# Transposing q and k of batches 2 to 7 by DMA instead of on TensorE, in an attention kernel fused with an expert layer

## Chip, cores, metric

One core of one Trainium2 chip. The metric is the device time of one launch in microseconds (us), the median of several executions. The profile is one execution, taken by the hardware profiler; its times count from the start of its own span.

## The reference

Sliding-window attention (window 128, ALiBi bias) over 8 batches of 8 heads, 576 positions, head size 64; its output, 4608 rows of 512, goes through a two-matrix layer with a gated activation.

```python
scores = (q @ k.T) / sqrt(64) + slope[h] * -(i - j)   # kept where 0 <= i - j < 128
x = softmax(scores) @ v                               # to rows of 512 = 8 heads x 64
h = x @ w_in                                          # 512 -> 2048
g = h * (1.0 / (1.0 + exp(-beta * h)))
out = g @ w_out                                       # 2048 -> 512, float32
```

## The kernel before

Each batch has five blocks of rows (128, 128, 128, 128, 64). A block of q and k is loaded as float32 rows into `fst`, cast to bf16 on GpSimd (`bst`), transposed on TensorE into PSUM, and copied by VectorE into `QK`, where the score matmuls read it. Batches alternate between two `QK` buffers. Each batch is done in two halves: blocks 0 to 2, then 3 and 4. GpSimd also casts v into `VS`.

```python
fst_pool = ctx.enter_context(tc.tile_pool(name="fst", bufs=16))
bst_pool = ctx.enter_context(tc.tile_pool(name="bst", bufs=4))
...
def load_qk(b, sb):
    rows = ROWS[sb]
    fq = load_rows(q, b, sb)          # nc.sync.dma_start, like every load and store here
    fk = load_rows(k, b, sb)
    t = bst_pool.tile([P, 2, H, D], BF16, name="bst", tag="bst")
    nc.gpsimd.tensor_copy(out=t[0:rows, 0], in_=fq[0:rows])
    c = nc.gpsimd.tensor_copy(out=t[0:rows, 1], in_=fk[0:rows])
    staged[b, sb] = t
...
def T(b, sb):
    rows = ROWS[sb]
    src = staged.pop((b, sb))
    tps = psum_t.tile([P, 2, NP, P], BF16, name="tps", tag="t")
    for i in range(2):
        for p in range(NP):
            nc.tensor.transpose(
                out=tps[:, i, p, :],
                in_=src[:, i, 2 * p : 2 * p + 2, :].rearrange("r h d -> r (h d)"),
                identity=ident[:],
            )
    nc.vector.tensor_copy(
        out=QK[b % 2][:, :, :, P * sb : P * sb + rows], in_=tps[:, :, :, 0:rows]
    )
...
def loads_ahead(b, m):
    if m == 0:
        if b:
            for sb in (3, 4):
                load_qk(b, sb)
            for sb in (2, 3, 4):
                load_v(b, sb)
    elif b + 1 < B:
        for sb in range(3):
            load_qk(b + 1, sb)
        for sb in range(2):
            c = load_v(b + 1, sb)
        if b == 0:
            ...                        # w_out, on another queue
```

TensorE's order is fixed by the program: for each group of 512 tokens, 16 steps `HS` (x by w_in into `hps`) alternate with 16 steps `OS` of the group before (`ops`), and pieces of the attention of the next group (transposes, scores `sps`, weights by v `pv`, transposes of x) are spread between them.

The softmax here doesn't subtract the row's maximum and nothing guards it: scores larger than these inputs give would overflow.

## Time and profile before

| | before |
|---|---|
| median time (3 runs) | 374.29 us |
| span of the profiled run (it took 376.31 us) | 374.6 us |
| first `ops` matmul on TensorE | 93.7 us |
| from there to the end | 280.9 us |
| q, k, v, weights read | 36.71 MB |

The prediction below shows how the profile is read: the slices for where the bound lies, the stretches for who sets the pace, the timeline for what a group costs. Three lines from the page and one from TensorE's timeline are added, because the result is measured against them.

```profile
PEclk9999999899999999999999999999999999999999
...
HBM read 36.71 MB, written 9.44 MB: 123 GB/s over the span
...
L96 POOL CAST bst<-fst 128x512 bf16<-128x512 f32 (+1 forms) x40 | 24.6, 615 | 108.8 <-issue 78.7
```

### The profile page before, as it was taken

What the parts mean: (1) busy time and instruction counts of PE and PEld (TensorE: products, weight loads), DVE (VectorE), ACT (ScalarE), POOL (GpSimd) and SP (SyncE); (2) the same over time, 40 slices, a digit from 0 to 9 for tenths busy, and PEclk for the clock granted to TensorE, in tenths of its full rate; (3) what the DMA queues carried; (4) which work ended last, traced back from release to release, by engine and by line L of the source; (5) the groups of instructions that cost most, each with busy time, mean ns of one, the idle gap of its engine ahead of it and who ended that gap; (6) DMA issues with size and microseconds to landing.
All of it is one profiled execution on the core that took longest, in us unless ns stands there. A gap on an engine that the chain in (4) does not pass through costs nothing.

```text
span 374.6 us, 6713 instructions
## 1 busy us (share of the span) xinstructions
PE 338.5 (90%) x2529; PEld 172.7 (46%) x2529; DVE 224.2 (60%) x473; ACT 214.4 (57%) x437; POOL 84.4 (23%) x151
## 2 busy tenths in 40 slices
PE   2367687788999999999999999999999999999995
PEld 1145334434454455445454545454545445544442
DVE  3266467777665677665666776776767755533400
ACT  1453359375745875585846694668566854445421
POOL 7570703453122213112033303320100000000000
PEclk9999999899999999999999999999999999999999
DMA  9999999999297898954138440000000010001012
GB/s 166 209 206 202 193 195 214 192 216 180 76 214 159 159 186 170 205 126 107 50 96 187 109 104 31 28 30 29 30 28 30 30 57 29 29 29 58 28 56 86
DMA packets 121985, 42.40 MB, mean 113 GB/s; under 512 B 113232, under 2 KB 117344, under 8 KB 121952
## 3 DMA queue, kind: packets, MB, share of 16 engines
q1 hardware_dynamic: 117728, 37.77, 47.9%
q0 software_dynamic: 4224, 4.19, 6.7%
q8 instruction: 20, 0.33, 0.4%
q14 instruction: 13, 0.11, 0.1%
HBM read 36.71 MB, written 9.44 MB: 123 GB/s over the span
## 4 chain that ended last, share of the span: by engine, by line
PE 80%; DMA 6%; DVE 4%; ACT 4%; SPq 4%; issue 1%; POOL 0%; ACTq 0%
PE ops L283 34%; PE hps L267 32%; PE sps L197 4%; DMA fst<-in_k_dram 4%; PE tps L171 4%; SPq L83 4%; ACT pt L207 3%; PE xt L249 2%; PE pv L233 2%; DVE gT L273 2%; PE pv L229 2%; DMA fst<-in_v_dram 1%; ACT sig L272 1%; DVE pt L211 1%; DVE qkT L176 1%
## 5 line engine op out<-in xcount | busy, mean ns | idle before, releaser
L272 ACT ACTIVATE sig<-hps,beta_h 128x512 bf16<-128x512 f32 x144 | 99.5, 692 | 98.4 <-PE hps L267 87.4
L267 PE MATMUL hps<-XT,W 128*128 128x512 bf16 x576 | 150.7, 385 | 3.6 <-DVE gT L273 3.0
L283 PE MATMUL ops<-W,gT 128*128 128x512 bf16 x576 | 144.9, 379 | 0.0
L273 DVE SCALAR_TENSOR_TENSOR gT<-sig,hps 128x512 bf16<-128x512 bf16 x144 | 98.3, 683 | 53.0 <-ACT sig L272 52.4
L207 ACT ACTIVATE pt<-sps,bias 128x256 bf16<-128x256 f32 (+2 forms) x256 | 100.4, 480 | 34.9 <-PE sps L197 34.6
L267 PEld LDWEIGHTS <-W 128*128 128x128 bf16 x576 | 51.1, 98 | 56.5 <-issue 10.9
L283 PEld LDWEIGHTS <-gT 128*128 128x128 bf16 x576 | 51.3, 98 | 52.2 <-issue 1.7
L211 DVE TENSOR_TENSOR pt<-pt,mask 128x1024 bf16<-128x1024 bf16 x64 | 46.1, 720 | 21.2 <-ACT pt L207 20.0
L96 POOL CAST bst<-fst 128x512 bf16<-128x512 f32 (+1 forms) x40 | 24.6, 615 | 108.8 <-issue 78.7
L197 PE MATMUL sps<-qkT 64*128 64x256 bf16 (+2 forms) x320 | 28.3, 271 | 14.1 <-ACT pt L207 13.1
L104 POOL CAST vs<-fst 128x512 bf16<-128x512 f32 (+1 forms) x40 | 26.1, 659 | 65.0 <-PE pv L233 38.1
L176 DVE COPY qkT<-tps 128x1024 bf16<-128x1024 bf16 (+1 forms) x40 | 25.5, 637 | 21.5 <-PE tps L171 21.3
L171 PE MATMUL tps<-ident,bst 128*128 128x128 bf16 x320 | 28.8, 240 | 7.8 <-POOL bst L96 4.3
L239 DVE TENSOR_TENSOR xn<-pv,zs 128x256 bf16<-128x256 f32 (+1 forms) x80 | 33.7, 422 | 2.6
L289 ACT ACTIVATE osb<-ops 128x512 f32<-128x512 f32 x36 | 21.6, 601 | 20.8 <-PE ops L283 20.8
L233 PE MATMUL pv<-vs,pt 128*128 128x65 bf16 x320 | 31.0, 200 | 2.5 <-DVE xn L239 1.5
L171 PEld LDWEIGHTS <-bst 128*128 128x128 bf16 x320 | 23.5, 107 | 17.3 <-POOL bst L96 4.9
L197 PEld LDWEIGHTS <-qkT 64*128 64x128 bf16 x320 | 12.4, 97 | 38.2 <-issue 35.1
L233 PEld LDWEIGHTS <-pt 128*128 128x128 bf16 x320 | 23.6, 102 | 13.7 <-issue 1.8
L97 POOL CAST bst<-fst 128x512 bf16<-128x512 f32 (+1 forms) x40 | 25.3, 634 | 9.3 <-DMA fst<-in_k_dram 9.2
L229 PE MATMUL pv<-vs,pt 128*128 128x65 bf16 x256 | 25.8, 200 | 1.8 <-DVE qkT L176 1.2
L229 PEld LDWEIGHTS <-pt 128*128 128x128 bf16 x256 | 21.3, 102 | 8.3 <-DVE xn L239 1.3
(26 smaller groups left out, 74.3 us busy)
## 6 DMA issues: line engine op xcount, KB each, us to landing
out_dram<-osb SPq DMA_DIRECT2D x36, 256.0 KB, 2.0
fst<-in_q_dram SPq DMA_DIRECT2D x32, 256.0 KB, 4.8
fst<-in_k_dram SPq DMA_DIRECT2D x32, 256.0 KB, 4.8
fst<-in_v_dram SPq DMA_DIRECT2D x32, 256.0 KB, 5.0
W<-in_moe_w_in_dram POOLq DMA_DIRECT2D x4, 512.0 KB, 11.5
W<-in_moe_w_out_dram POOLq DMA_DIRECT2D x4, 512.0 KB, 12.6
fst<-in_q_dram SPq DMA_DIRECT2D x8, 128.0 KB, 4.2
fst<-in_k_dram SPq DMA_DIRECT2D x8, 128.0 KB, 4.2
```

The source lines that it names most:

```text
L171: nc.tensor.transpose(out=tps[:, i, p, :], in_=src[:, i, 2 * p : 2 * p + 2, :].rearrange("r h d -> r (h d)"), identity=ident[:],)
L176: nc.vector.tensor_copy(out=QK[b % 2][:, :, :, P * sb : P * sb + rows], in_=tps[:, :, :, 0:rows])
L197: nc.tensor.matmul(o, lhsT=qk[64 * e : 64 * e + 64, 1, p, P * kb : P * kb + P], rhs=qk[64 * e : 64 * e + 64, 0, p, P * kb : P * kb + nq], ...
L207: nc.scalar.activation(out=pt[:, e, cols], in_=sps[:, e, cols], func=ACTF.Exp, scale=qscale, bias=bias[:, half, h : h + 1],)
L211: nc.vector.tensor_tensor(out=pt[:], in0=pt[:], in1=masks[m][:], op=ALU.mult)
L229: nc.tensor.matmul(pv[:, hl, 0 : D + 1], lhsT=weights(b, qb - 1, h, 1), rhs=vs[:, qb - 1, h, 0 : D + 1], start=True, stop=False,)
L233: nc.tensor.matmul(pv[:, hl, 0 : D + 1], lhsT=weights(b, qb, h, 0), rhs=vs[:, qb, h, 0 : D + 1], start=qb == 0, stop=True,)
L239: nc.vector.tensor_tensor(out=xn[0:nq, 4 * g : 4 * g + 4, :], in0=pv[0:nq, :, 0:D], in1=zs[0:nq].broadcast_to([nq, 4, D]), op=ALU.mult,)
L267: nc.tensor.matmul(hps[:], lhsT=W1[:, c, bass.ts(j, P)], rhs=XT[:, c, c0 : c0 + TOKG], start=(c == 0), stop=(c == NDM - 1),)
L272: nc.scalar.activation(out=sig[:], in_=hps[:], func=ACTF.Tanh, scale=beta_h[:, j : j + 1])
L273: nc.vector.scalar_tensor_tensor(out=gts[g][:, j, :], in0=sig[:], scalar=1.0, in1=hps[:], op0=ALU.add, op1=ALU.mult)
L283: nc.tensor.matmul(ops_[:], lhsT=gT[:, j, i * P : i * P + P], rhs=W2[:, j, :], start=(j == 0), stop=(j == NFF - 1),)
```

## The change

Its intent: TensorE sets the pace from 94 us on, so take q's and k's transposes off it. From batch 2 on each block is transposed by two DMAs on the load queue, straight into `QK`, half a batch before the scores need it. The loads move half a batch ahead in the program for that, and three f32 buffers become bf16 buffers.

```diff
+    NPE = 2
-    fst_pool = ctx.enter_context(tc.tile_pool(name="fst", bufs=16))
-    bst_pool = ctx.enter_context(tc.tile_pool(name="bst", bufs=4))
+    fst_pool = ctx.enter_context(tc.tile_pool(name="fst", bufs=13))
+    bst_pool = ctx.enter_context(tc.tile_pool(name="bst", bufs=7))
@@ def T(b, sb)
+        if b >= NPE:
+            for i in range(2):
+                nc.sync.dma_start_transpose(
+                    out=QK[b % 2][:, i, :, P * sb : P * sb + rows],
+                    in_=src[0:rows, i].rearrange("r h d -> r (h d)"),
+                )
+            return
@@ the pieces of one half
-            a = [(None, lambda b=b, sb=sb: T(b, sb)) for sb in ((0, 1, 2), (3, 4))[m]]
+            ts = [(b, (0, 1, 2)), (b, (3, 4))][m : m + 1] if b < NPE else []
+            nb, nm = (b, 1) if m == 0 else (b + 1, 0)
+            if NPE <= nb < B:
+                ts.append((nb, ((0, 1, 2), (3, 4))[nm]))
+            a = [(None, lambda b=b, sb=sb: T(b, sb)) for b, sbs in ts for sb in sbs]
@@ def loads_ahead(b, m), the new body (cut: the old lines)
+        if b == 0 and m == 1:
+            for sb in range(3):
+                load_qk(1, sb)
+            for sb in range(2):
+                c = load_v(1, sb)
+            ...                                   # w_out as before
+            for sb in (3, 4):
+                load_qk(1, sb)
+        elif b and m == 0:
+            for sb in (2, 3, 4):
+                load_v(b, sb)
+            if b + 1 < B:
+                for sb in range(3):
+                    load_qk(b + 1, sb)
         elif b + 1 < B:
+            for sb in range(2):
+                load_v(b + 1, sb)
+            for sb in (3, 4):
                 load_qk(b + 1, sb)
```

More of the change, by code (lines that the diff above doesn't have):

```diff
@@ L335, in loads_ahead @@
     def loads_ahead(b, m):
-        if m == 0:
-            if b:
-                for sb in (3, 4):
-                    load_qk(b, sb)
-                for sb in (2, 3, 4):
-                    load_v(b, sb)
+        if b == 0 and m == 1:
[3 more added lines that the diff above has]
+                c = load_v(1, sb)
+            with tc.issue_after(c.ins):
+                for n in range(4):
+                    load_w2(n)
+            for sb in (3, 4):
[6 more added lines that the diff above has]
+                    load_qk(b + 1, sb)
         elif b + 1 < B:
-            for sb in range(3):
+            for sb in range(2):
+                load_v(b + 1, sb)
+            for sb in (3, 4):
                 load_qk(b + 1, sb)
-            for sb in range(2):
-                c = load_v(b + 1, sb)
-            if b == 0:
-                with tc.issue_after(c.ins):
-                    for n in range(4):
-                        load_w2(n)
     with tc.manual_schedule(engines={mybir.EngineType.PE}):
```

## The prediction

> **What bounds the kernel now.** I read the page's busy shares and forty slices first, then a table of stretches, then TensorE's timeline inside one stretch, the costliest groups, the chain that ended last, and at the end the timelines of the load queue and of the casts around the place where the change begins.
>
> ```profile
> PE 338.5 (90%) x2529; PEld 172.7 (46%) x2529; DVE 224.2 (60%) x473; ACT 214.4 (57%) x437; POOL 84.4 (23%) x151
> ...
> PE   2367687788999999999999999999999999999995
> ...
> DMA  9999999999297898954138440000000010001012
> ...
> L176 DVE COPY qkT<-tps 128x1024 bf16<-128x1024 bf16 (+1 forms) x40 | 25.5, 637 | 21.5 <-PE tps L171 21.3
> L171 PE MATMUL tps<-ident,bst 128*128 128x128 bf16 x320 | 28.8, 240 | 7.8 <-POOL bst L96 4.3
> ```
>
> The slices split the run in two. Up to slice 10 (94 us) TensorE has gaps and the DMA engines are full. From there to the end TensorE has none, while the DMA engines empty from slice 17 on. A table of 40 us stretches says the same in microseconds (columns: busy and count of PE, PEld, DVE, ACT, POOL, then granted clock, DMA share, GB/s):
>
> ```profile
> 95.00:135.00 40.00, 40.00 (x318) 20.27 (x317) 24.65 (x53) 24.63 (x53) 9.90 (x17) 1.00 0.76 159
> ...
> 175.00:215.00 40.00, 40.00 (x317) 20.26 (x316) 27.23 (x57) 26.13 (x54) 9.08 (x15) 1.00 0.48 118
> ```
>
> PE 40.00 of 40, VectorE and ScalarE near 27: TensorE sets the pace. The busy figure of a group overstates what it costs there, because matmuls overlap in the pipeline; the cost is the step from one group's start to the next one's. TensorE's timeline shows it:
>
> ```profile
> 196.34 1.02 PE L267 MATMUL hps<-XT,W 128*128 128x512 bf16 x4
> 197.20 0.61 PE L171 MATMUL tps<-ident,bst 128*128 128x128 bf16 x8
> 197.65 1.03 PE L283 MATMUL ops<-W,gT 128*128 128x512 bf16 x4
> 198.51 0.19 PE L229 MATMUL pv<-vs,pt 128*128 128x65 bf16 x1
> ```
>
> One block's eight transposes hold TensorE from 197.20 to 197.65, so 0.45 us (56 ns each), not the 8 x 240 ns = 1.92 us of the group's mean, nor the 0.61 that the line gives. In the first part of the run it is the chain that counts, here around the second half of batch 2:
>
> ```profile
> 87.30 1.02 PE hps L267 x4
> 88.32 0.46 PE tps L171 x8
> 88.78 0.02 issue
> 88.81 0.69 DVE qkT L176
> 89.50 0.60 DVE gT L273
> ```
>
> There TensorE waits for VectorE (gT frees the PSUM buffer of hps), and the copy of the transposed block stands in front of gT on VectorE: transpose and copy together are 1.15 us of the path.
>
> **What the Trainium skill says.** "VectorE: DVE Perf Modes", section "The three transpose paths", gives a 128x128 bf16 transpose 390 ns on TensorE and 1309 ns by DMA. The trace has 219 ns as the length of one and 56 ns as its pitch, so in a stream TensorE is far cheaper than the page's figure and the gain must be sized from the trace. "DMA: Bandwidth & Descriptors", section "Latency and other measured facts", gives 261 GB/s for a DMA transpose with a non-contiguous middle dimension; "Advanced Engine Details and Errata", section "X-Bar Transpose (TRN2)", says they are as fast as ordinary DMAs. The trace of before has no such transfer, so neither is confirmed; its own loads run at about 200 GB/s when the engines are full. The DMA page's section "Issuing engines are not separate DMA queues" says that transfers from any queue share the same 16 engines; the trace agrees at least in that loads of 5 us take 16.5 us (a k load at 22.39 in the chain) while the weights come in on another queue.
>
> **The change part by part.**
>
> Removed from TensorE: 6 batches x 5 blocks x 8 = 240 of the 320 transposes, 30 blocks x 0.45 us = 13.5 us. Batches 3 to 7 have their transposes at 105 us and after, in the stretch with no gap: 25 x 0.45 = 11.3 us, which should come off the end one for one. Batch 2's five blocks (at 63 to 73 and 88 to 91 us) lie in the part with gaps.
>
> Removed from VectorE: 24 copies of 690 ns and 6 of 424 ns = 19.1 us. Behind the full TensorE (VectorE 27 of 40) they are worth nothing. For batch 2 they are worth what the chain holds of them: the two blocks near 90 us are 1.15 and 0.88 us, and the three before add a copy of 0.61 us at 72.16 and TensorE steps of about 0.5 us each at 67.73 and 70.69. That is 3.6 us; since something else will often take the place of a removed link, I count 2.5 us.
>
> Added: 60 DMA transposes on the load queue, 54 equivalents of 128x512 bf16 (131 KB). At 261 GB/s one takes 0.50 us, 27 us in all, an estimate from the page's figure. A batch then asks of the DMA engines 3.54 MB of f32 loads (17.7 us at 200 GB/s), 1.18 MB of transposes (4.5 us) and about 4.5 stores of under 1 us: some 26 us, against a batch period of 37 to 40 us in the trace (first transposes of batches 5, 6, 7 at 191, 229, 267 us). So it fits in the steady state, with half a batch (18 us) for load queue, transfer and landing. Of the sequencer that issues: a load takes it 0.37 us when the engines are free and about 1.1 us when they are full. I assume 1.3 us for a transpose (the page's 1309 ns, as an estimate of one that isn't pipelined): 10 x 1.3 + 15 loads x 0.7 + 5 stores x 0.4 = 25 us per batch. Also fits.
>
> Moved: loads keep their linear order (q and k of one half, v of the half between); only their place in the program is half a batch earlier. Three of the 16 f32 buffers become bf16 buffers; 13 x 1.3 us of loads in flight is still 17 us, above the 4.8 us from issue to landing, so I count nothing.
>
> The one place that I expect to hurt is the beginning of batch 2, the first to use the new path while the DMA engines are still full (columns: start, length; first the cast, then the load queue, then TensorE):
>
> ```profile
> 66.49 0.61 POOL L97 CAST bst<-fst 128x512 bf16<-128x512 f32 x1 [0.48 <-DMA fst<-in_k_dram]
> ```
> ```profile
> 67.42 1.10 SPq L83 DMA_DIRECT2D fst<-in_q_dram  x1
> 68.62 0.60 SPq L83 DMA_DIRECT2D fst<-in_k_dram  x1
> ```
> ```profile
> 72.47 0.62 PE L197 MATMUL sps<-qkT 64*128 64x256 bf16 x4
> ```
>
> The last cast of batch 2's first three blocks ends at 67.1; the loads that stand before the transposes in program order are issued until 69.2; the scores start at 72.47. Six transposes at 1.3 us of issue are out at 69.2 + 7.8 = 77.0, and land perhaps 4 us later (as the loads do), so the scores would start at 81 if all six stood in a row behind the loads and at 72 if the first ones were put between. I take the middle, 4 us, as lost: TensorE works in order, and nothing later gives it back.
>
> Sum: 374.3 - 11.3 - 2.5 + 4.0 = 364.5 us.
>
> **The rivals.**
>
> (a) *All of it hidden:* the transposes go out as soon as each cast is done and batch 2 is not late. For: casts run well ahead from 78 us on, where they wait for TensorE to free a bf16 buffer (6.3 us). Against: the zero slack at 61 to 72 us. Then 374.3 - 13.8 = 360.5, and 357 if VectorE's relief shortens more of the early chain.
>
> (b) *The load queue becomes the bound.* It issues in order: loads, transposes that wait for a cast, and stores that wait for ScalarE. From 62 to about 105 us it would have 21 loads at 1 us and 16 transposes at 1.3 us, 42 us, so batch 3 would be just in time too; stores in the same queue could hold transposes and be held by them. For: before, between 92 and 100 us, all loads stood behind the first store and DMA share was near nothing. Against: later the loads are a batch ahead. Each late half costs 2 to 5 us; with two or three late, 368 to 373.
>
> (c) *The transpose is slow:* if the page's 1309 ns hold for each 128x128 and four of them go one after the other, one instruction is 5.2 us and a batch needs 9 x 5.2 = 47 us of the queue, more than the batch period. The kernel would be paced by it, at 374 + 6 x 10 or so, over 400 us. The bandwidth figures on the other two pages speak against it; no trace here does.
>
> (d) *TensorE freed, another engine takes over:* without the transposes a batch has about 36 us of TensorE, and VectorE and ScalarE some 25 and 26 us in it. A bound by either would need alternation stalls through the single score buffer; but the transposes stand in other slots than the scores, so the score steps keep their spacing. I count at most 2 us.
>
> **Range and chances.** The middle is 364.5. Low end 357 from (a). High end 375 from (b) at its worst with gains cancelled. The border of faster is 374.3 x 0.98 = 366.8, only 2.3 us above the middle, and the largest unknown, the late start of batch 2 (0 to 9 us), lies across it. Faster 0.58; within 2% 0.33, mostly (b); slower 0.09, nearly all (c) and a worse form of (b).
>
> **What would show it.** In the profile of the changed kernel: 80 transposes left on TensorE and 10 copies on VectorE; from about 100 us to the end TensorE with no gap, and the batch period shorter by 5 x 0.45 = 2.25 us, 36 in place of 38; a wait of TensorE's scores on a DMA that writes qkT once, near 72 us, of some 4 us; transposes in the DMA table with a landing time of 3 to 6 us; DMA share up by about a tenth between 100 and 300 us. It would be wrong if scores wait for the transposed blocks in every half (then b or c), if one transpose holds the issuing queue for well over 1.3 us, if stores leave late and ScalarE waits for their buffers, or if gaps in front of hps from ScalarE or VectorE appear in the stretch after 100 us (then d).

## More of the kernel before

Group 0 has no `OS` to go with it, so the first `ops` matmul marks the end of the start-up.

```profile
93.71 1.02 PE L283 MATMUL ops<-W,gT 128*128 128x512 bf16 x4
```

The first gives TensorE's granted clock in tenths; it dips once, in slice 7 (66 to 75 us). 40 casts are 8 batches of 5 blocks.

## The result

| | before | after |
|---|---|---|
| median time (4 runs each) | 374.54 us | 378.54 us |
| first `ops` matmul | 93.7 us | 108.3 us |
| from there to the end | 280.9 us | 269.7 us |

The ratio is 1.0115, with a 95% interval of 1.008 to 1.015: within 2%, but slower, and outside the predicted range. The result passes the comparison with the reference.

The page of the kernel after, the lines that answer to those shown of before:

```profile
PE 324.5 (86%) x2248; PEld 158.7 (42%) x2289; DVE 209.3 (55%) x443; ACT 214.4 (57%) x437; POOL 90.0 (24%) x157
...
PE   2365577608789999999999999999999999999996
...
PEclk9999999966999999999999999999999999999999
DMA  9999999999998899988987889850000011001012
...
HBM read 38.02 MB, written 9.44 MB: 126 GB/s over the span
...
L97 POOL CAST bst<-fst 128x512 bf16<-128x512 f32 (+1 forms) x42 | 26.5, 631 | 51.9 <-DMA fst<-in_q_dram 36.4
...
L179 PE MATMUL tps<-ident,bst 128*128 128x128 bf16 x80 | 10.6, 292 | 12.3 <-POOL bst L97 8.8
```

and one from its table of DMA issues (count, median us from issue to landing):

```profile
qkT<-bst SPq DMA_TRANSPOSE x60, 2.9
```

Three things are to be seen. TensorE lost 240 transposes and is full from slice 12 on. One slice of the start-up (8, 76 to 85 us) has a 0 for TensorE, and its clock is down to six tenths in that slice and the next. And the kernel reads 1.31 MB more than before, with 42 casts where 40 are needed.

The DMA sequencer's timeline after (start, length, what), and TensorE's in the same stretch:

```profile
75.42 0.81 SPq L84 DMA_DIRECT2D fst<-in_k_dram  x1
76.41 8.84 SPq L171 DMA_TRANSPOSE qkT<-bst  x6
85.30 2.07 SPq L84 DMA_DIRECT2D fst<-in_v_dram  x3
```

```profile
72.79 1.02 PE L275 MATMUL hps<-XT,W 128*128 128x512 bf16 x4
...
81.81 0.40 PE L205 MATMUL sps<-qkT 64*128 64x256 bf16 x2 [8.00 <-DMA qkT<-bst]
85.85 0.40 PE L205 MATMUL sps<-qkT 64*128 64x256 bf16 x2 [3.65 <-DMA qkT<-bst]
...
89.84 1.90 PE L275 MATMUL hps<-XT,W 128*128 128x512 bf16 x4
...
108.31 1.03 PE L291 MATMUL ops<-W,gT 128*128 128x512 bf16 x3
```

The brackets are idle time and its releaser. The first scores of batch 2 wait 8.00 and 3.65 us for transposed blocks, and four `hps` matmuls that took 1.02 us before the wait take 1.90 after it. The whole run has only these two waits of a TensorE matmul on a DMA into `qkT`. So the account divides cleanly at the first `ops` matmul: the start-up lost 14.6 us, the rest gained 11.2 us. The profiled runs lie above their medians, before by 2.0 us and after by 1.1. The rest lasts 280.9 us in each of the three profiles without DMA transposes (before and experiments 2 and 5), so this scatter lies in the start-up, and differences of start-up times between profiles are good to 1 or 2 us.

The theory (A) at this point: the start-up lost to two causes. First, in the first half of batch 0 the new load plan falls through to its last branch (b = 0, m = 0 meets neither condition before it, and b + 1 < B holds), so two blocks of v and two of q and k of batch 1 are loaded, and then loaded again in the second half. Second, batch 2's transposes come late, because they stand behind loads in the one queue. The rivals: (B) the doubled loads are hidden and the smaller f32 pool costs time; (C) the place in the queue does not matter, because the transposes are slow while the DMA engines are full.

### The profile page after: what moved, and what is told of

The parts are those of the page before. It is cut to its first block, busy times and chain, and to the rows that moved or that the text cites. A ratio compares the mean times of both kernels' runs of the same rounds, so it can differ in the third digit from the quotient of the medians. Undisturbed runs are those within 1.5% of the kernel's fastest.

```text
span 378.0 us, 6264 instructions
## 1 busy us (share of the span) xinstructions
PE 324.5 (86%) x2248; PEld 158.7 (42%) x2289; DVE 209.3 (55%) x443; ACT 214.4 (57%) x437; POOL 90.0 (24%) x157
## 4 chain that ended last, share of the span: by engine, by line
PE 73%; DMA 17%; SPq 3%; POOL 2%; ACT 2%; issue 1%; DVE 1%; ACTq 0%; POOLq 0%
PE ops L291 33%; PE hps L275 30%; DMA fst<-in_k_dram 11%; PE sps L205 4%; DMA fst<-in_v_dram 3%; SPq L84 3%; PE pv L241 2%; PE xt L257 2%; PE pv L237 2%; DMA fst<-in_q_dram 1%; DMA qkT<-bst 1%; DVE gT L281 1%; ACT pt L215 1%; ACT sig L280 1%; POOL bst L98 1%
## 5 line engine op out<-in xcount | busy, mean ns | idle before, releaser
L275 PE MATMUL hps<-XT,W 128*128 128x512 bf16 x552 | 149.0, 387 | 5.8 <-DVE gT L281 3.8
L291 PE MATMUL ops<-W,gT 128*128 128x512 bf16 x559 | 142.2, 379 | 1.0 <-issue 0.3
L219 DVE TENSOR_TENSOR pt<-pt,mask 128x1024 bf16<-128x1024 bf16 x64 | 47.9, 748 | 16.2 <-ACT pt L215 15.8
L105 POOL CAST vs<-fst 128x512 bf16<-128x512 f32 (+1 forms) x42 | 27.1, 653 | 88.4 <-DMA fst<-in_v_dram 71.9
L97 POOL CAST bst<-fst 128x512 bf16<-128x512 f32 (+1 forms) x42 | 26.5, 631 | 51.9 <-DMA fst<-in_q_dram 36.4
L246 DVE RECIPROCAL zs<-pv 128x4 f32<-128x4 f32 (+1 forms) x80 | 14.2, 178 | 36.4 <-PE pv L241 34.6
L98 POOL CAST bst<-fst 128x512 bf16<-128x512 f32 (+1 forms) x42 | 26.8, 638 | 19.7 <-DMA fst<-in_k_dram 18.5
L262 DVE COPY XT<-xt 128x512 bf16<-128x512 bf16 (+1 forms) x40 | 15.6, 390 | 12.7 <-PE xt L257 12.0
L179 PE MATMUL tps<-ident,bst 128*128 128x128 bf16 x80 | 10.6, 292 | 12.3 <-POOL bst L97 8.8
## 6 DMA issues: line engine op xcount, KB each, us to landing
W<-in_moe_w_in_dram POOLq DMA_DIRECT2D x4, 512.0 KB, 11.9
```

The lines of the kernel that those rows point to most:

```text
L105: return nc.gpsimd.tensor_copy(out=VS[b % 2][0:rows, sb, :, 0:D], in_=f[0:rows])
L219: nc.vector.tensor_tensor(out=pt[:], in0=pt[:], in1=masks[m][:], op=ALU.mult)
L275: nc.tensor.matmul(hps[:], lhsT=W1[:, c, bass.ts(j, P)], rhs=XT[:, c, c0 : c0 + TOKG], start=(c == 0), stop=(c == NDM - 1),)
L291: nc.tensor.matmul(ops_[:], lhsT=gT[:, j, i * P : i * P + P], rhs=W2[:, j, :], start=(j == 0), stop=(j == NFF - 1),)
```

## The experiments

All ten results passed the comparison with the reference, number 4 too, which uses wrong q and k: with q and k drawn at 0.1 the scores are small beside the bias, so passing says little of the transposes themselves. Kernels of one group shared their runs of the kernel before (medians 375.19, 374.82 and 375.35 us in the three groups).

**1. Blocks loaded once.**

```diff
-        elif b + 1 < B:
+        elif b and b + 1 < B:
```

> The changed kernel, with the blocks that it loads twice loaded once (in the first half of batch 0 its load plan also loads four blocks of batch 1, two of v and two of q and k, which are then loaded again; the page of after shows 42 casts of each kind and 38.0 MB read where before had 40 and 36.7). Theory A (the 14.6 us lost up to the first output matmul, at 108.3 us against 93.7, are two things: 1.31 MB loaded for nothing while the DMA engines are full, at 200 GB/s 6.5 us, and the transposes of batch 2 that stand behind loads in the queue): the first output matmul moves from 108 to about 102 us and the time from 378.5 to 372. Rival B (the loss is the late transposes and the smaller pool of f32 buffers alone; the doubled loads are hidden): 377 to 379.

Measured: 373.68 us, ratio to before 0.9954 (0.9914 to 0.9995). HBM reads are back at 36.71 MB and the first `ops` matmul is at 101.9 us. The doubled loads cost 4.9 us of the time. The late batch 2 stays as it was, only earlier:

```profile
69.95 9.80 SPq L171 DMA_TRANSPOSE qkT<-bst  x6
```

```profile
66.99 1.02 PE L275 MATMUL hps<-XT,W 128*128 128x512 bf16 x4
76.01 0.40 PE L205 MATMUL sps<-qkT 64*128 64x256 bf16 x2 [8.00 <-DMA qkT<-bst]
80.28 0.40 PE L205 MATMUL sps<-qkT 64*128 64x256 bf16 x2 [3.87 <-DMA qkT<-bst]
```

TensorE stands ready for the scores at 68.0; the casts were done by then, as in before, but the queue reaches the first transpose only at 69.95 and is at the six of them for 9.80 us, a pitch of 1.63 (one by one they hold it 1.19 to 2.29 us; 0.5 us of the stretch is a wait).

**2. The kernel before, with the doubled loads.**

```diff
             if b:
                 ...
+            else:
+                for sb in range(2):
+                    load_v(1, sb)
+                for sb in (3, 4):
+                    load_qk(1, sb)
```

> The kernel before, with the same four blocks of batch 1 loaded twice at the same place of the program, and nothing else changed. Theory A: the loads that follow are 6 us later, batch 1 and 2 start later by that, and the time goes from 374.5 to about 380. Rival B: 374 to 376, since the loads run a batch ahead later on.

Measured: 380.48 us, ratio 1.0137 (1.0095 to 1.018). Put alone into the old kernel, the doubled loads cost 5.3 us between the medians.

```profile
97.66 1.03 PE L283 MATMUL ops<-W,gT 128*128 128x512 bf16 x4
```

The first `ops` matmul is 4.0 us later than in before, and the stretch after it lasts 280.9 us, as before: the whole loss stays in the start-up. B's first half falls.

**3. Blocks loaded once, DMA transposes from batch 3 on.**

```diff
-    NPE = 2
+    NPE = 3
-        elif b + 1 < B:
+        elif b and b + 1 < B:
```

> The changed kernel with the doubled loads taken out and the DMA transposes begun at batch 3 in place of 2, so that batch 2 goes through TensorE as before. Theory A (from 100 us on the DMA transposes are hidden and 25 blocks x 0.45 us are saved): first output matmul near 94 us as before, 374.5 - 11.3 = 363. If batch 3 were as late as batch 2 (the queue is the bound): 368 to 372, with a wait of the scores on the DMA into qkT of several us.

Measured: 364.88 us, ratio 0.9717 (0.9672 to 0.9762), faster by 2.8%.

```profile
87.24 8.54 SPq L171 DMA_TRANSPOSE qkT<-bst  x6
```

```profile
91.56 1.89 PE L291 MATMUL ops<-W,gT 128*128 128x512 bf16 x8
```

The queue takes as long over six transposes as before, but now no TensorE matmul waits for a block transposed by DMA in the whole run, and the rest of the run lasts 270.5 us. The same slow issue is hidden once there is slack. Moving one batch back was worth 8.8 us against experiment 1.

**4. No transposes for batch 2** (wrong: its scores read what batch 0 left).

```diff
+        if b == 2:
+            return
         if b >= NPE:
```

> The changed kernel without any transposes for batch 2 (wrong on purpose: its scores use what batch 0 left in the buffer), doubled loads kept. Theory A: the two waits of the scores on the DMA into qkT (8.0 and 3.65 us) go, some us of half clock after them too, and ten transposes of 1.2 to 1.4 us leave the load queue: 364 to 367. Rival (the scores would wait there anyway for something else, the loads or ScalarE): 373 to 377.

Measured: 366.66 us, ratio 0.9764 (0.9716 to 0.9812; at 2% unclear). With the doubled loads kept, taking the late data away is worth 11.9 us, so nothing else held the scores there. It takes more than the wait away (ten DMAs of the queue, and the scores' need of batch 2's q and k loads), so it is a bound and no version to use.

**5. The kernel before with the changed pools** (13 f32 and 7 bf16 buffers).

```diff
-    fst_pool = ctx.enter_context(tc.tile_pool(name="fst", bufs=16))
-    bst_pool = ctx.enter_context(tc.tile_pool(name="bst", bufs=4))
+    fst_pool = ctx.enter_context(tc.tile_pool(name="fst", bufs=13))
+    bst_pool = ctx.enter_context(tc.tile_pool(name="bst", bufs=7))
```

> The kernel before with the changed pools alone: 13 buffers for f32 blocks in place of 16, 7 for bf16 blocks in place of 4. If the smaller pool of f32 buffers is part of the early loss (theory B), 377 or more. If not (theory A): 373 to 376.

Measured: 375.06 us, ratio 0.9987 (0.9931 to 1.0044). The pools cost nothing that this shows; the rest of B falls.

**6. Transposes in front of the half's loads** (blocks loaded once, from batch 2).

```diff
-            att.append((None, lambda b=b, m=m: loads_ahead(b, m)))
+            ds = [(b, sb) for b, sbs in ts for sb in sbs if b >= NPE]
+            att.append((None, lambda b=b, m=m, ds=ds: [T(*d) for d in ds] + [loads_ahead(b, m)]))
```

(An empty entry stays where each transpose stood, so that TensorE's order does not change.)

> The changed kernel with blocks loaded once, and in each half the DMA transposes put in front of that half's loads in the program (behind them before), everything else in its place. If batch 2 is late because its transposes stand behind four q and k loads and two v loads in the one queue (theory A, place in the queue): the queue reaches them as the casts end, at 62 to 68 us, the scores' waits of 8.0 and 3.9 us shrink to 1 to 5 us together, and the time goes from 373.7 to 365 to 369. Rival (place does not matter, the transposes are slow in the DMA engines while these are full, or the loads held back by them are then late in turn): 372 to 376.

Measured: 366.03 us, ratio 0.9756 (0.9708 to 0.9803; at 2% unclear, by a hair).

```profile
62.89 7.17 SPq L171 DMA_TRANSPOSE qkT<-bst  x5
70.12 1.50 SPq L84 DMA_DIRECT2D fst<-in_v_dram  x1
71.73 1.20 SPq L171 DMA_TRANSPOSE qkT<-bst  x1
```

```profile
69.47 0.28 PE L205 MATMUL sps<-qkT 64*128 64x256 bf16 x2
72.69 0.40 PE L205 MATMUL sps<-qkT 64*128 64x256 bf16 x2 [2.93 <-DMA qkT<-bst]
```

The queue starts on the transposes 7 us earlier than in experiment 1; of 11.9 us of waits one of 2.93 is left, and 7.7 us of the time come back. The transposes are nearly as slow as before (a pitch of 1.43 us against 1.63) and the DMA engines nearly as full (share 0.81 over the five, 0.84 over the six of experiment 1), so C falls as the main cause: most of batch 2's lateness is the place in the queue. The wait that is left is hold and transfer: the fifth transpose is issued at 68.86, behind four others, and lands 3.79 us later. (A load of v stands before the sixth, though the program puts all six in front. The wait ends with the fifth, so this load is not behind it.)

**7. q and k of a block in one DMA** (blocks loaded once, from batch 2, old place).

```diff
-            for i in range(2):
-                nc.sync.dma_start_transpose(
-                    out=QK[b % 2][:, i, :, P * sb : P * sb + rows],
-                    in_=src[0:rows, i].rearrange("r h d -> r (h d)"),
-                )
+            nc.sync.dma_start_transpose(
+                out=QK[b % 2][:, :, :, P * sb : P * sb + rows].rearrange("p i n c -> p (i n) c"),
+                in_=src[0:rows].rearrange("r i h d -> r (i h d)"),
+            )
```

> The changed kernel with blocks loaded once, and q and k of a block transposed by one DMA of 128x1024 in place of two of 128x512: 30 instructions, the same bytes. The queue was held 1.2 to 1.6 us by each of 60. If that is a cost of the instruction: 1.2 to 1.6 us for each of 30, batch 2's six take 4.5 in place of 9.8 us, the second wait of its scores shrinks by 3 to 4 us and the time goes from 373.7 to about 369. If it is a cost of the bytes: 2.4 to 3 us each, no change, 373 to 374.5.

Measured: 371.52 us, ratio 0.9894 (0.9842 to 0.9947), 2.2 us below experiment 1.

```profile
71.15 4.60 SPq L170 DMA_TRANSPOSE qkT<-bst  x3
```

```profile
76.65 0.40 PE L204 MATMUL sps<-qkT 64*128 64x256 bf16 x2 [9.11 <-DMA qkT<-bst]
77.95 0.40 PE L204 MATMUL sps<-qkT 64*128 64x256 bf16 x2 [0.90 <-DMA qkT<-bst]
```

Three DMAs of twice the bytes take the queue 4.60 us where six took 9.80. Over this range the hold belongs to the instruction, not to the bytes. The second wait shrinks by 3.0 us as expected; the first does not, since the first transpose still stands behind the loads. It even grows by 1.1 us, as the queue comes to the transposes 1.2 us later, so the time misses the 369 expected. The hold is a part of the lateness, then, but the smaller one.

**8. DMA transposes from batch 3 on, doubled loads kept.**

```diff
-    NPE = 2
+    NPE = 3
```

> The changed kernel with the DMA transposes begun at batch 3 and nothing else changed, so with the blocks loaded twice. If the two causes add (doubled loads about 5 to 6 us, late batch 2 about 9 us): 378.5 - 9 = 369 to 371.

Measured: 370.37 us, ratio 0.9869 (0.9822 to 0.9916). With experiments 1 and 3 and the kernel after this makes a square (medians, of runs in three groups whose before differs by 0.6 us): the doubled loads cost 4.9 us with batch 2 by DMA and 5.5 with it on TensorE; batch 2 by DMA costs 8.2 and 8.8. The two causes add.

**9. Early place and joined DMAs, from batch 2:** the edits of numbers 1, 6 and 7 together.

```diff
+            att.append((None, lambda b=b, m=m, ds=ds: [T(*d) for d in ds] + [loads_ahead(b, m)]))
+            nc.sync.dma_start_transpose(... "p i n c -> p (i n) c" ... "r i h d -> r (i h d)" ...)
```

> Blocks loaded once, DMA transposes in front of the half's loads, and q and k of a block in one DMA. Place and number of instructions together: the one wait left in the run with the early place (2.9 us, on the last block of the first half of batch 2) shrinks by 1 to 2 us, and loads stand behind 15 in place of 30 transposes per three batches: 363 to 365.5. If the last cast, and not the queue, sets that wait: 365.5 to 366.5, as with the early place alone.

Measured (5 rounds): 366.57 us, ratio 0.976 (0.9724 to 0.9796). No gain over the early place alone: the wait left is 3.9 us, not less. With the transposes in front the queue comes to the last one just after its cast (cast done at 67.54, issue at 67.67), and the rest of the wait is its transfer: it lands 5.39 us later. Joining saves only issue time.

**10. The same from batch 3.**

```diff
-    NPE = 2
+    NPE = 3
```

> The same with the DMA transposes begun at batch 3. Batch 2's five blocks are on TensorE and VectorE again, in the part with gaps. If batch 2 by DMA now gains its 2.5 us of the early chain: this is 1 to 3 us slower than the version from batch 2, 365 to 367. If that part is paced by the loads whichever way: equal or faster, 362.5 to 365.

Measured (5 rounds): 365.08 us, ratio 0.9743 (0.9701 to 0.9785). Together with experiments 3 and 6 this leaves four versions between 364.9 and 366.6 us whose intervals overlap (at 2% number 6 is unclear, the others are faster); which is the best is not settled. The simplest that beats both kernels is number 3: load once, begin at batch 3.

## Why the prediction was wrong

**Right: what TensorE saves.** The step of 25 blocks x 0.45 us = 11.3 us: the part after the first `ops` matmul went from 280.9 to 269.7 us, 11.2 less. In the ten experiments the part is 269.8 to 270.7 us wherever the DMA transposes are in (10.2 to 11.1 less), and 280.9 in both where they are not. Reading the cost as the step from start to start was the right way; the mean of 240 ns in the group would have promised 48 us. (No run moves the loads without the transposes; but TensorE is full in this part of both kernels, so earlier loads could not have shortened it.)

**Right: rivals (c) and (d) fail.** The median of a transpose on the queue is 1.21 us, with a pitch of 1.4 to 1.6 when the queue is full, against 1.3 assumed, and 2.9 us to landing. Experiment 1 has TensorE without a gap (40.00 of 40, three times over) from 120 to 240 us, so neither ScalarE nor VectorE took over.

**Wrong: "loads keep their linear order ... only their place in the program is half a batch earlier".** This step of the part "Moved" failed on the diff, not on the chip. I read the three branches as a reshuffle and did not run the first call, b = 0 and m = 0, through them. It cost 4.9 to 5.5 us of time. A count of the blocks that each call loads, against 40 of each kind, would have shown it, and 1.31 MB at the 200 GB/s that the prediction itself used is 6.5 us in a part it called full.

**Wrong: "I take the middle, 4 us, as lost".** Mechanism, place and start time were right: the transposes do begin behind the loads, at 69.95 us in experiment 1 against 69.2 in the working. But the working had two ends, scores at 72 if some transposes went first and at 81 if all stood in a row, and I averaged them with no evidence for the better one. The queue keeps the order of the program here: all in a row, the last scores released at 80.28. The loss was also counted from the scores' old start at 72.47, though without the transposes TensorE stood ready at 68.0. So the two waits are 8.0 + 3.9 = 11.9 us where 4 was counted. In the prediction's sum batch 2 cost 4.0 - 2.5 = 1.5 us; measured, it costs 8.2 to 8.8.

**A term left out: the clock.** In experiment 1 the granted clock is 0.57 from 70 to 75 us, 0.50 to 80 and 0.57 to 85, then full. The Trainium skill's page "TensorE: Matmul & The Clock Gate", section "Part 1: The HAM clock gate", says that the array falls to half clock after an idle window of about 3.4 us and recovers after one that is busy. The trace agrees on the half and on the way back (full at 84.3, some 4 us after the scores start), but not on the length of the window: the clock is halved at 70.7, 2.7 us after TensorE's last matmul; in experiment 6 at 72.1, 2.3 us after it; in before at 67.6, with no gap above 1.2 us in the 4 us in front. Four `hps` matmuls take 1.90 us just after the wait and 1.02 before it. I put this at about 2 us, an estimate from the 4 us of matmuls done at half rate. The profile of before is at half clock from 67.6 to 71.0 as well, so the net term is smaller; no run separates it from the wait.

**Not settled: "I count 2.5 us" for VectorE's relief.** Part of it can be seen. From the first eight `hps` matmuls after batch 2's first scores to the first `ops` matmul it is 16.3 us with batch 2 on TensorE (before, 77.36 to 93.71; experiment 3, 75.23 to 91.56) and 15.6 with it by DMA (experiment 1, 86.36 to 101.94; experiment 6, 78.48 to 94.08); the other runs have 16.3 to 16.8 and 15.6 to 15.8. So the two blocks of the second half are worth about 0.75 us, where the working had 1.15 + 0.88. The chain that ended last shows why: `sig` on ScalarE (0.70 us) and `gT` on VectorE (0.70) take the place of the transpose and the copy. For the whole start-up experiments 4 and 8 give an upper bound, since neither waits for a DMA into `qkT`: 95.3 against 98.0, 2.7 us (3.7 in the medians). Between 0.8 us and that bound the size stays open. (The working's two TensorE steps of "about 0.5 us" are 0.80 and 0.58 in the trace, the first at half clock.) The loads do not pace this part: the chain of before has no transfer in it from 60 us on.

**Rival (b)** was the nearest, but one late half sufficed, not "two or three": the later ones had slack.

In the prediction's terms, from the medians: batches 3 to 7 by DMA gave 10.3 us (experiment 3 against its before; 11.3 predicted), batch 2 by DMA cost 8.8 (1.5 predicted), the doubled loads 4.9 (not foreseen). 374.5 - 10.3 + 8.8 + 4.9 = 377.9, where 378.5 was measured; the rest is the drift of before between the groups. This splits the measured difference and is no second check of it.

## What to carry to other kernels

Moving work from a full engine to a queue pays where the queue has slack, and the first unit moved is the one to check: here one batch too early cost 8 of the 11 us that five batches saved. Where work is put in an in-order queue, write down who stands in front of it and take the program's order as the order until a trace shows better. When a diff reorders loads, count what each call of the loader loads, first and last call included; the bytes read on the page of the profile (36.7 against 38.0 MB) show such a slip at once.

## What the Trainium skill lacked or had wrong

- "DMA: Bandwidth & Descriptors", section "Issuing engines are not separate DMA queues", calls the sequencer's time to initiate a DMA "usually small relative to the DMA itself". For these transposes it is what counts: each holds the queue 1.2 us or more, so in the kernel after six of 128x512 took 8.8 us for 0.79 MB, 89 GB/s, and no load went out meanwhile.
- The same page has no measured time for the hold by a transpose from SBUF to SBUF of this size on trn2 (it has sequencer cycles, for other sizes). Here the hold is per instruction over this range: one DMA of 128x1024 has a median of 1.28 us on the queue against 1.21 for 128x512, and three in a row took 4.6 us where six of half the size took 9.8 (experiments 7 and 1).
- That page's section "Latency and other measured facts" gives 261 GB/s for a DMA transpose with a non-contiguous middle dimension; by it 128x512 would take 0.50 us, an estimate. On the load queue the packets took 54.9 us more of the 16 engines in experiment 1 than in before (63.0% of 371.9 us against 47.9% of 374.6). If all of it is put down to the 54 such transposes, that is 1.0 us each, or 129 GB/s, next to loads.
- "As fast as regular DMAs" ("Advanced Engine Details and Errata", section "X-Bar Transpose (TRN2)") is not seen either: by the same measure the load queue of before moves 37.77 MB in 179.4 us, 210 GB/s. Per packet the two are near: 24 ns in before, and 30 ns for the 548 packets that each transpose adds. No run has transposes with the DMA engines to themselves.
- "VectorE: DVE Perf Modes", section "The three transpose paths": 390 ns for a 128x128 transpose on TensorE. The trace has 219 ns for one and 56 ns from one to the next, which that section does not give, and the latter is what taking it away gives back (11.2 us for 200 of them).
- "TensorE: Matmul & The Clock Gate", section "Part 1: The HAM clock gate": the idle window of about 3.4 us is longer than what the traces show. The clock was halved 2.3 and 2.7 us after the last matmul (experiments 6 and 1), and in before after gaps of 1.2 and 0.8 us alone.
